# Linear attention and an ELU block on one core: scores of two heads as 64-row tiles, K^T V kept dense, both halves of a tile in one place

## The chip, the core and the metric

The kernel runs on one core of a Trainium2 chip. Its engines work side by side, each on its own queue of instructions and in order: PE (TensorE, matrix products), ACT (ScalarE), DVE (VectorE), POOL (GpSimd) and SP (which only starts transfers here). The metric is the time of one execution on the device in microseconds, from the median of several runs.

## The reference

```python
kv  = einsum('bhsd,bhse->bhde', k, v)          # 8 batches, 8 heads, 576 rows, head size 64
o   = einsum('bhsd,bhde->bhse', q, kv)
o   = o / sqrt(mean(o*o, over e) + 1e-6) * g_norm
x   = o with its heads side by side            # 4608 rows of 512
h   = x @ w_in                                 # 512 x 2048
g   = h if h > 0 else exp(h) - 1
out = g @ w_out                                # 2048 x 512
```

Inputs and output are float32; the kernel multiplies in bfloat16 and accumulates in float32.

## The kernel before, in words

The rows are worked off in nine tiles of 512. Tiles 0 to 7 take the first 512 rows of a batch each; tile 8 takes the last 64 rows of all eight batches. For each tile T there is an *attention* (its x, turned so that features lie on partitions: `xT`), a *first product* (h by eight steps `mm1`, each of eight matmuls that fill two banks of an accumulator `h_ps`), an *elu* (exponential on ACT, then `rest` on DVE: a step with min and subtract on `elu_e`, and one that takes the maximum with `h_ps` into `gT`), and a *second product* (`mm2`: 16 matmuls for each of four groups of 128 rows into `o_ps`, then a copy on ACT and a store from SP). With `relu` in an elu ACT also writes the positive part as bfloat16 (`elu_h`), which frees `h_ps` earlier, and DVE adds two bfloat16 operands.

Attention of tile T (function `attention`, line 249) is cut into pieces that the order of the program places among the steps of tile T-1's products:

- `kv` (`kv_single`, line 171): K^T V of batch T on PE, 72 matmuls of 64 rows by 64 columns. Two heads that share a pair (index l) stand on the two halves of the partitions. `kv_out` (line 352) casts the result with ACT into `bd_kv`, a block-diagonal tile: each pair of heads has a 128x128 block, of which the two off-diagonal quarters are zero. It takes one cast for each half of the partitions. The zeros come from a memset on DVE at the start (line 509).
- `qd` (line 261): a transposing transfer from SP that makes `qT`, queries with two heads on 128 partitions.
- `se0`, `se1` (`se_mm`, line 202): scores, here the product of q with K^T V, for 256 rows each. One matmul takes 128 partitions of `qT` (two heads) and a block of `bd_kv`, so that a matmul serves two heads at once, with half of what it multiplies being zeros. Eight matmuls fill the two banks of the accumulator `at`. In tile 8 each matmul has 64 output rows, since every 64 rows have their own batch. The same piece squares the result on ACT (line 227).
- `sum`, `inv`, `mul`: sums of squares by head on DVE (L232), logarithm and exponential on ACT for the root (L238, L239), and `scale_rows` on DVE (line 241), which writes `xs` in bfloat16.
- `xd0`, `xd1` (line 322): transposing transfers from SP of `xs` into `xT`; `xg0`, `xg1` (line 332) multiply `xT` by the gain vector on DVE. Attentions 1 and 2 use PE transposes instead (`x0`, `x1`, line 295). Tile 0 has a path of its own at the start, without `bd_kv`; a copy on POOL (L677) puts its K^T V there for tile 8.

The accumulator memory has eight banks: one tile `at` of two banks (pool `ps_at`, one buffer), two buffers of two banks for h (`ps_m1`), two of one bank for the second product (`ps_m2`). A pool hands out its buffers in turn, and the writer of a buffer waits for the last reader of the one before.

The order of each engine is the order in which the program is written (the kernel schedules by hand). `group` (line 728) writes out tiles 2 to 8: for i from 0 to 7 the i-th `mm1` of tile T, a piece of `mm2` of tile T-1, the `rest` of the elu, and the attention pieces whose start is i. From tile 3 on, the first eight matmuls of `mm2` stand ahead of the group, and the other seven pieces at i = 0 to 6. The starts are

```python
start = {"kv": 0, "se0": 1, "xd0": 2, "se1": 3, "xd1": 4, "xg0": 5, "xg1": 6}
```

with sum and inv of a half one step after its scores, and mul ahead of the other pieces there. Tile 1 is written out ahead of it (lines 757 to 777): attention 2 has `se0` after the seventh `mm1`, `se1` after eight matmuls of the second product. POOL's queue fetches q, k and v of later batches, each behind a small copy that waits for `qd`'s landing.

Of the kernel before, what the change touches and what calls it, by code (L numbers as in the profile page):

```python
# [8 lines left out]
FP32 = mybir.dt.float32  # L9
BF16 = mybir.dt.bfloat16  # L10
AF = mybir.ActivationFunctionType
ALU = mybir.AluOpType
# [4 lines left out]
def kernel(  # L17
# [13 lines left out]
    nc = tc.nc  # L31
    P = 128

    B, H, S, D = q.shape
    DM = H * D
# [25 lines left out]
    nc.vector.memset(eps_col, 1e-6)  # L61
    bd_kv = const.tile([P, B, NPAIR, P], BF16, name="bd_kv")

# [103 lines left out]
    def at_tile(dtype):  # L167
        full = ps_at.tile([P, 1024], FP32, name="at", tag="at")
        return full if dtype == FP32 else full.bitcast(BF16)
# [31 lines left out]

    def se_mm(T, j, qT, se_ps):

        ov = se_ps.rearrange("p (u l s e) -> p u l s e", u=2, l=2, s=2)
        for p in range(NPAIR):
            s, u = p // 2, p % 2
            if T < B:
                nc.tensor.matmul(  # L208
                    ov[:, u, :, s, :],
                    lhsT=qT(p, j),  # L210
                    rhs=bd_kv[:, T, p, :],
                    start=True,
                    stop=True,
                )
            else:
                for l in range(2):
                    nc.tensor.matmul(  # L217
                        ov[l * 64 : l * 64 + 64, u, :, s, :],
                        lhsT=qT(p, j)[:, l * 64 : l * 64 + 64],
                        rhs=bd_kv[:, 2 * j + l, p, :],  # L220
                        start=True,
                        stop=True,
                    )

# [15 lines left out]

    def scale_rows(xs, se_ps, ss, n):
        nc.vector.tensor_tensor(  # L242
            out=xs.rearrange("p c (h e) -> p (c h) e", h=H),
            in0=se_ps.rearrange("p c (h e) -> p (c h) e", h=H),
            in1=ss.to_broadcast([P, n * H, D]),
            op=ALU.mult,
        )

    def attention(T):
# [19 lines left out]

        def se(h):  # L270


            def product(se_ps=None):
                if se_ps is None:
                    se_ps = at_tile(FP32).rearrange("p (c f) -> p c f", c=2)
                for c in range(2):
                    se_mm(T, 2 * h + c, st["qT"], se_ps[:, c, :])
                st["se", h] = se_ps
                st["sq", h] = square(se_ps, 2)

            def sums():
                st["ss", h] = sum_heads(st.pop(("sq", h)), 2)

            def inv():
                inv_rms(st["ss", h])

            def scale():
                if h == 0:
                    st["xs"] = attp.tile([P, J, DM], BF16, name="xs", tag="xs")
                rows = st["xs"][:, 2 * h : 2 * h + 2, :]  # L290
                scale_rows(rows, st.pop(("se", h)), st.pop(("ss", h)), 2)

            return product, sums, inv, scale

# [57 lines left out]
        def kv_out(us):  # L352
            bd_v = bd_kv[:, T].rearrange("p (s u) e -> p s u e", s=2)
            for l in range(2):
                ls = slice(l * 64, l * 64 + 64)
                nc.scalar.copy(  # L356
                    bd_v[ls, :, us, ls],
                    st["kv"][ls, :, 0:P].rearrange("p s (u e) -> p s u e", u=2)[:, :, us],
                )

# [6 lines left out]

        pieces = {"kv": kv_all, "q": q_t, "qd": q_dma}
        pieces["landed"] = lambda: after(st["at"])
# [5 lines left out]
        for h in range(2):  # L375
            for name, piece in zip(("se", "sum", "inv", "mul"), se(h)):
                pieces[f"{name}{h}"] = piece
# [85 lines left out]
    def mm2_quarter(T, j, i):  # L463
        mm2(T, j, 4 * i, 4 * i + 4)
# [43 lines left out]
    nc.vector.memset(one, 1.0)  # L508
    nc.vector.memset(bd_kv, 0.0)
    fetch_q(0)  # L510
# [158 lines left out]
    for i in range(2, 8):  # L669
# [3 lines left out]
        if i == 5:  # L673
            at["q"]()
    for l in range(2):
        ls = slice(l * 64, l * 64 + 64)
        nc.gpsimd.tensor_copy(  # L677
            out=bd_kv[ls, 0].rearrange("p (s u) e -> p u s e", s=2)[:, :, :, ls], in_=kv0[ls]
        )
    load_w_out(3)  # L680
# [12 lines left out]
    at["kv1"]()  # L693
    at["se0"]()
    at["se1"](wide)
    for n in range(2):
# [30 lines left out]

    def group(T, at, start, second, relu=()):


        early, late = {}, {}
        for name, i in start.items():
            if name in ("se0", "se1"):
                early.setdefault(i + 1, []).extend(("sum" + name[2], "inv" + name[2]))
                late.setdefault(i + 1, []).insert(0, "mul" + name[2])
            late.setdefault(i, []).append(name)
        for i in range(9 if 8 in early else 8):
            if i == 8:
                for name in early[8] + late[8]:
                    at[name]()  # L740
                break
            rest = mm1(
                T, i, (slice(0, 512),), i in relu, between=[at[name] for name in early.get(i, ())]
            )
            for piece in second.get(i, ()):
                mm2(*piece)
            names = late.get(i, [])
            if i in relu and names[:1] in (["mul0"], ["mul1"]):
                at[names.pop(0)]()
            rest()  # L750
            for name in names:
                at[name]()

# [4 lines left out]
    for i in range(8):  # L758
        rest = mm1(1, i, relu=i in (1, 4), spare=i in (2, 5))
        rest()  # L760
        if i == 3:
            at["kv"]()
        if i == 6:
            at["se0"]()
    mm2(1, 0, 0, 8)
    at["se1"](ps_m1.tile([P, 2, G], FP32, name="se_ps", tag="mm1"))
    for n in range(2):
# [5 lines left out]
    mm2(1, 1, 0, FC)  # L773
    at["x0"]()
    at["x1"](ps_m1.tile([P, 2, G], FP32, name="xt_ps", tag="mm1")[:, 0, :])
    mm2_quarter(1, 2, 0)
    mm2_quarter(1, 2, 1)

    for T in range(2, NT):
        second = {i: [(T - 1, i // 2, 8 * (i % 2), 8 * (i % 2) + 8)] for i in range(8)}  # L780
        if T > 2:
            mm2(*second[0][0])
            second = {i - 1: second[i] for i in range(1, 8)}
        else:
            quarters = [(1, 2 + i // 4, 4 * (i % 4), 4 * (i % 4) + 4) for i in range(2, 8)]
            second = {i + 1: [piece] for i, piece in enumerate(quarters)}
        at, start = ahead, {}
        if T + 1 < NT:
            start = {"kv": 0, "se0": 1, "xd0": 2, "se1": 3, "xd1": 4, "xg0": 5, "xg1": 6}
        if T + 2 < NT:  # L790
            at["landed"]()
            fetch(T + 2)
            ahead = attention(T + 2)
        group(T, at, start, second, (1, 2, 4) if T == 2 else ())
        if T + 2 < NT:
            ahead["qd"]()
# [48 lines left out]
```

## Time and profile before

| what | us |
|---|---|
| median of 6 runs | 287.15 (286.98 to 287.46) |
| the profiled execution, its own time | 286.98 |
| its span, first to last instruction | 285.2 |
| PE busy | 277.6 |
| DVE busy | 168.3 |
| ACT busy | 144.0 |
| POOL busy | 53.1 |

The granted clock of PE is 0.999 of its full speed. Lines of the profile name the source line, the engine, the operation, the written and read tiles and their shapes; a number of instructions stands behind an x, then busy time and the mean length of one, then the time in which the engine was idle before them and what ended it. Matmuls overlap, so the mean length of one (379 ns for 512 moving columns) is more than the distance between two starts. PEld is the loading of the stationary operand, which runs beside PE. In this chip's profile K^T V is L177, the scores are L208 (L217 in tile 8), h is L399 and the second product L446 (L804 for the last tile).

### The profile page before, as it was taken

What the parts mean: (1) busy time and instruction counts of PE and PEld (TensorE: products, weight loads), DVE (VectorE), ACT (ScalarE), POOL (GpSimd) and SP (SyncE); (2) the same over time, 40 slices, a digit from 0 to 9 for tenths busy, and PEclk for the clock granted to TensorE, in tenths of its full rate; (3) what the DMA queues carried; (4) which work ended last, traced back from release to release, by engine and by line L of the source; (5) the groups of instructions that cost most, each with busy time, mean ns of one, the idle gap of its engine ahead of it and who ended that gap; (6) DMA issues with size and microseconds to landing.
All of it is one profiled execution on the core that took longest, in us unless ns stands there. A gap on an engine that the chain in (4) does not pass through costs nothing.

```text
span 285.2 us, 4859 instructions
## 1 busy us (share of the span) xinstructions
PE 277.6 (97%) x2001; PEld 133.3 (47%) x2001; DVE 168.3 (59%) x220; ACT 144.0 (50%) x205; POOL 53.1 (19%) x94
## 2 busy tenths in 40 slices
PE   6999899999999999999999999999999999999994
PEld 2544454445544444445444544454444444444444
DVE  5459461778378657655865577547764776444400
ACT  3779554785486455335543454455434553333311
POOL 7835302431431231005100520011000000000000
PEclk9999999999999999999999999999999999999999
DMA  7999999796992597168915892545150213010122
GB/s 198 206 204 203 206 205 165 222 170 126 180 175 57 150 176 173 37 149 113 239 37 151 106 227 56 150 98 153 34 143 16 97 28 99 0 76 0 74 74 74
DMA packets 55961, 35.96 MB, mean 126 GB/s; under 512 B 32772, under 2 KB 53508, under 8 KB 55940
## 3 DMA queue, kind: packets, MB, share of 16 engines
q0 software_dynamic: 20192, 17.30, 39.3%
q1 hardware_dynamic: 35348, 17.83, 24.3%
q10 hardware_dynamic: 400, 0.52, 0.5%
q8 instruction: 15, 0.25, 0.3%
q14 instruction: 6, 0.05, 0.1%
HBM read 36.70 MB, written 9.44 MB: 162 GB/s over the span
## 4 chain that ended last, share of the span: by engine, by line
PE 88%; DMA 10%; issue 0%; ACT 0%; POOLq 0%
PE h_ps L399 39%; PE o_ps L446 39%; DMA w_out_sb<-in_moe_w_out_dram 6%; PE o_ps L804 5%; DMA w_in_sb<-in_moe_w_in_dram 3%; DMA k_pk<-in_k_dram 2%; PE at L208 2%; PE at L177 2%; PE at L306 0%; PE at L217 0%; PE se_ps L208 0%; ACT bd_kv L356 0%; PE xt_ps L306 0%; ACT o_last L812 0%; POOLq L829 0%
## 5 line engine op out<-in xcount | busy, mean ns | idle before, releaser
L399 PE MATMUL h_ps<-xT,w_in_sb 128*128 128x512 bf16 x560 | 130.9, 379 | 0.0
L446 PE MATMUL o_ps<-w_out_sb,gT 128*128 128x512 bf16 x512 | 120.5, 379 | 0.2 <-DMA w_out_sb<-in_moe_w_out_dram 0.2
L411 ACT ACTIVATE elu_e<-h_ps 128x1024 bf16<-128x1024 f32 (+1 forms) x75 | 73.0, 982 | 81.8 <-PE h_ps L399 80.1
L399 PEld LDWEIGHTS <-w_in_sb 128*128 128x128 bf16 x560 | 53.5, 98 | 62.0 <-issue 0.2
L430 DVE TENSOR_TENSOR gT<-elu_e,h_ps 128x1024 bf16<-128x1024 bf16 (+1 forms) x66 | 76.3, 1156 | 6.9
L446 PEld LDWEIGHTS <-gT 128*128 128x128 bf16 x512 | 49.8, 98 | 59.3 <-DMA w_out_sb<-in_moe_w_out_dram 0.3
L422 DVE TENSOR_SCALAR elu_e<-elu_e 128x1024 bf16<-128x1024 bf16 (+1 forms) x76 | 32.2, 423 | 71.2 <-ACT elu_e L411 71.1
L459 ACT COPY o_sb<-o_ps 128x512 f32<-128x512 f32 x32 | 18.6, 587 | 16.6 <-PE o_ps L446 16.6
L232 DVE TENSOR_REDUCE ss<-sq 128x16 f32<-128x1024 bf16 x16 | 19.3, 1218 | 9.0 <-ACT sq L227 9.0
L227 ACT ACTIVATE sq<-at 128x1024 bf16<-128x1024 f32 x14 | 14.3, 1024 | 12.4 <-PE at L208 9.9
L151 POOL COPY q_bf<-q_pk 128x512 bf16<-128x512 bf16 x24 | 14.5, 632 | 28.0 <-DMA q_pk<-in_q_dram 28.0
L242 DVE TENSOR_TENSOR xs<-at,ss 128x1024 bf16<-128x1024 f32 x14 | 17.1, 1218 | 1.2 <-ACT ss L239 1.2
L804 PE MATMUL o_ps<-w_out_sb,gT 128*128 128x512 bf16 (+1 forms) x80 | 14.1, 337 | 0.0
L125 POOL COPY gate<-qT 1x1 bf16<-1x1 bf16 x6 | 1.2, 194 | 63.9 <-DMA qT<-q_bf 63.9
L104 POOL DMA_DIRECT2D q_pk<-in_q_dram x14 | 10.6, 765 | 3.1 <-issue 1.8
L804 PEld LDWEIGHTS <-gT 128*128 128x128 bf16 x80 | 7.7, 98 | 6.4 <-DVE gT L430 0.4
L118 POOL DMA_DIRECT2D k_pk<-in_k_dram x12 | 8.3, 694 | 5.3 <-DMA w_in_sb<-in_moe_w_in_dram 2.5
L417 ACT ACTIVATE elu_h<-h_ps 128x1024 bf16<-128x1024 f32 x9 | 9.2, 1019 | 0.0
L208 PEld LDWEIGHTS <-qT 128*128 128x128 bf16 x112 | 7.3, 98 | 3.5 <-issue 0.5
L118 POOL DMA_DIRECT2D v_pk<-in_v_dram x12 | 8.3, 689 | 2.3 <-DMA w_in_sb<-in_moe_w_in_dram 1.8
L177 PEld LDWEIGHTS <-k_pk 64*64 64x64 bf16 x576 | 6.5, 107 | 4.0 <-issue 3.8
L527 PE MATMUL bank<-zeros 128*128 128x512 bf16 x19 | 6.8, 487 | 1.2 <-DVE zeros L502 1.2
(71 smaller groups left out, 112.4 us busy)
## 6 DMA issues: line engine op xcount, KB each, us to landing
out_dram<-o_sb SPq DMA_DIRECT2D x16, 512.0 KB, 3.0
q_pk<-in_q_dram POOLq DMA_DIRECT2D x14, 256.0 KB, 5.6
k_pk<-in_k_dram POOLq DMA_DIRECT2D x6, 576.0 KB, 8.4
v_pk<-in_v_dram POOLq DMA_DIRECT2D x6, 576.0 KB, 10.5
w_in_sb<-in_moe_w_in_dram POOLq DMA_DIRECT2D x4, 512.0 KB, 10.6
w_out_sb<-in_moe_w_out_dram POOLq DMA_DIRECT2D x4, 512.0 KB, 15.1
st_q<-in_q_dram SPq DMA_DIRECT2D x2, 512.0 KB, 4.6
st_q<-in_q_dram SPq DMA_DIRECT2D x16, 64.0 KB, 2.5
```

The source lines that it names most:

```text
L118: nc.gpsimd.dma_start(out=raw[name, b].rearrange("p h j d -> p h (j d)")[:, hs], in_=in_[:, hs])
L151: eng.tensor_copy(out=out_, in_=in_)
L227: nc.scalar.activation(sq, se_ps, AF.Square)
L232: nc.vector.reduce_sum(out=ss, in_=sq.rearrange("p c (h e) -> p (c h) e", h=H), axis=AX.X)
L242: nc.vector.tensor_tensor(out=xs.rearrange("p c (h e) -> p (c h) e", h=H), in0=se_ps.rearrange("p c (h e) -> p (c h) e", h=H), in1=ss.to_b ...
L399: nc.tensor.matmul(h_ps[a][:, cs], lhsT=w_in_sb[:, c, f * P : f * P + P], rhs=x(c, cs), start=(c == 0), stop=(c == KC - 1),)
L411: nc.scalar.activation(e[:, lo:hi, :], ps, AF.Exp)
L422: nc.vector.tensor_scalar(out=e[:, lo:hi, :], in0=e[:, lo:hi, :], scalar1=1.0, scalar2=1.0, op0=ALU.min, op1=ALU.subtract,)
L430: nc.vector.tensor_tensor(out=gT[T][:, 2 * i + lo : 2 * i + hi, :], in0=e[:, lo:hi, :], in1=h, op=ALU.add if relu else ALU.max,)
L446: nc.tensor.matmul(o_ps[T, j], lhsT=gT[T][:, f, j * P : j * P + P], rhs=w_out_sb[:, f, :], start=(f == 0), stop=(f == FC - 1),)
L459: nc.scalar.copy(o_sb[T][:, j % 2, :], o_ps.pop((T, j)))
L804: nc.tensor.matmul(ps, lhsT=gT[B][:, f, j * P : j * P + P], rhs=w_out_sb[:, f, cols], start=(f == 0), stop=(f == FC - 1),)
```

## The change

`bd_kv` becomes `kv_sb`, which holds K^T V without zeros: 64 columns for each pair, one head on each half of the partitions. `kv_out` is one cast over 128 partitions, POOL's copy for tile 0 is one instruction, and the memset is gone. A scores matmul now takes one head: 64 partitions of `qT` and 64 columns of `kv_sb`; the two heads of a pair write to two different banks. The output is ordered by head within the pair first, so `scale_rows` works in two instructions for each half and sorts the columns while it writes `xs`.

In tiles 3 to 7 both halves of the scores stand together, after the fourth `mm1`: one half in `at`, the other in the two banks of the second product, which ACT copies to `se_sb` at once; no piece of `mm2` stands at that step, and one more at the last. Sums, roots, scaling and the two transfers all stand at i = 4, the gain multiplications at i = 6 and 7. The elu of steps 4 and 5 uses `relu` there. In tile 1 both halves stand where `se1` stood, and the second set of PE transposes moves one quarter of `mm2` later. Tile 2 keeps its order. The diff, cut:

```diff
-    bd_kv = const.tile([P, B, NPAIR, P], BF16, name="bd_kv")
+    kv_sb = const.tile([P, B, NPAIR, D], BF16, name="kv_sb")
...
+    def se_mm(T, h, qT, banks):
+        for jj in range(2):
+            j = 2 * h + jj
+            for p in range(NPAIR):
+                s, u = p // 2, p % 2
+                for t in range(1 if T < B else 2):
+                    rows = slice(0, P) if T < B else slice(t * 64, t * 64 + 64)
+                    for l in range(2):
+                        ls = slice(l * 64, l * 64 + 64)
+                        nc.tensor.matmul(
+                            banks[l].rearrange("p (j u s e) -> p j u s e", j=2, u=2, s=2)[
+                                rows, jj, u, s, :
+                            ],
+                            lhsT=qT(p, j)[ls, rows],
+                            rhs=kv_sb[ls, T if T < B else 2 * j + t, p, :],
+                            start=True,
+                            stop=True,
+                        )
...
-    def scale_rows(xs, se_ps, ss, n):
-        nc.vector.tensor_tensor(
-            out=xs.rearrange("p c (h e) -> p (c h) e", h=H),
-            in0=se_ps.rearrange("p c (h e) -> p (c h) e", h=H),
-            in1=ss.to_broadcast([P, n * H, D]),
-            op=ALU.mult,
-        )
+    def scale_rows(xs, se, ss):
+        for l in range(2):
+            nc.vector.tensor_tensor(
+                out=xs.rearrange("p j (u l s e) -> p l j u s e", u=2, l=2, s=2)[:, l].rearrange(
+                    "p j u s e -> p (j u) s e"
+                ),
+                in0=se[:, l, :].rearrange("p (a s e) -> p a s e", s=2, e=D),
+                in1=ss[:, 8 * l : 8 * l + 8]
+                .rearrange("p (a s) -> p a s", s=2)
+                .to_broadcast([P, 4, 2, D]),
+                op=ALU.mult,
+            )
...
+        def se(homes):
+            for h, home in homes.items():
+                if home is None:
+                    home = at_tile(FP32).rearrange("p (l f) -> p l f", l=2)
+                pair = isinstance(home, list)
+                banks = home if pair else [home[:, l, :] for l in range(2)]
+                se_mm(T, h, st["qT"], banks)
+                if pair:
+                    home = attp.tile([P, 2, G], FP32, name="se_sb", tag="se_sb", bufs=1)
+                    for l in range(2):
+                        nc.scalar.copy(home[:, l, :], banks[l])
+                st["se", h] = home
...
         def kv_out(us):
-            bd_v = bd_kv[:, T].rearrange("p (s u) e -> p s u e", s=2)
-            for l in range(2):
-                ls = slice(l * 64, l * 64 + 64)
-                nc.scalar.copy(
-                    bd_v[ls, :, us, ls],
-                    st["kv"][ls, :, 0:P].rearrange("p s (u e) -> p s u e", u=2)[:, :, us],
-                )
+            nc.scalar.copy(
+                kv_sb[:, T].rearrange("p (s u) e -> p s u e", s=2)[:, :, us],
+                st["kv"][:, :, 0:P].rearrange("p s (u e) -> p s u e", u=2)[:, :, us],
+            )
...
-    nc.vector.memset(bd_kv, 0.0)
...
+    def group(T, at, lead, second, relu=()):
+        for piece in lead:
+            mm2(T - 1, *piece)
...
+        for i in range(8):
+            between = [at["sq1"], at["sum0"], at["inv0"], at["sum1"]] if at and i == 4 else ()
+            rest = mm1(T, i, relu=i in relu, between=between)
+            if at and i == 3:
+                at["se"]({0: None, 1: [ps_m2.tile([P, DM], FP32, name="se_ps", tag="mm2") for _ in range(2)]})
+                at["sq0"]()
             for piece in second.get(i, ()):
-                mm2(*piece)
+                mm2(T - 1, *piece)
+            if at and i == 4:
+                at["inv1"]()
+                for n in range(2):
+                    at[f"mul{n}"]()
+                    at[f"xd{n}"]()
             rest()
+            if at and i == 0:
+                at["kv"]()
+            if at and i > 5:
+                at[f"xg{i - 6}"]()
...
-        if i == 6:
-            at["se0"]()
     mm2(1, 0, 0, 8)
-    at["se1"](ps_m1.tile([P, 2, G], FP32, name="se_ps", tag="mm1"))
+    at["se"]({0: None, 1: ps_m1.tile([P, 2, G], FP32, name="se_ps", tag="mm1")})
+    for n in range(2):
+        at[f"sq{n}"]()
...
     at["x0"]()
+    mm2_quarter(1, 2, 0)
     at["x1"](ps_m1.tile([P, 2, G], FP32, name="xt_ps", tag="mm1")[:, 0, :])
-    mm2_quarter(1, 2, 0)
     mm2_quarter(1, 2, 1)
...
+        elif T < B:
+            lead, pieces, steps = halves[:1], halves[1:], (0, 1, 2, 4, 5, 6, 7)
+        else:
+            lead, pieces, steps = halves[:1], halves[1:], range(7)
+        second = {i: [piece] for i, piece in zip(steps, pieces)}
+        group(T, at, lead, second, {2: (1, 2, 4), B: ()}.get(T, (4, 5)))
```

## The prediction

> **What bounds the kernel now.** I read the busy shares first, then the chain that ended last, then that chain in order of time, then the groups.
>
> ```profile
> PE 277.6 (97%) x2001; PEld 133.3 (47%) x2001; DVE 168.3 (59%) x220; ACT 144.0 (50%) x205; POOL 53.1 (19%) x94
> ...
> PE 88%; DMA 10%; issue 0%; ACT 0%; POOLq 0%
> ```
>
> TensorE is the bound, and ACT and DVE have half their time free. The chain in time (start, length, what) says where the changed parts sit on it:
>
> ```profile
> 34.40 0.45 PE at L177 x36
> ...
> 35.14 0.27 ACT bd_kv L356
> ...
> 35.45 0.61 PE at L208 x8
> 36.06 0.45 PE se_ps L208 x8
> 36.51 5.19 PE o_ps L446 x24
> ...
> 98.80 0.71 PE at L177 x72
> 99.50 1.83 PE h_ps L399 x8
> ...
> 219.70 0.57 PE at L217 x16
> 220.27 1.83 PE h_ps L399 x8
> ```
>
> From 30.8 us on PE runs without a gap, except 0.65 us at 34.8 for the two casts of K^T V. So the end moves by what PE's own work gets shorter, less any new wait. Eight matmuls of scores take 0.45 us (56 ns each, no loss on either side). Around the 64-row products (L177) and the 64-column ones (L217) time is lost: the next h_ps row is 1.83 instead of 1.73. The groups of matmuls and weight loads, kept apart by shape:
>
> ```profile
> L208 PE MATMUL at<-bd_kv,qT 128*128 128x128 bf16 x96 | 7.3, 219 | 0.6 <-ACT bd_kv L356 0.6
> L177 PE MATMUL at<-v_pk,k_pk 64*64 64x64 bf16 x504 | 5.7, 194 | 0.0
> L217 PE MATMUL at<-bd_kv,qT 128*64 128x128 bf16 x32 | 1.3, 222 | 0.0
> ...
> L208 PEld LDWEIGHTS <-qT 128*128 128x128 bf16 x112 | 7.3, 98 | 3.5 <-issue 0.5 <-PE at L177 0.2
> L217 PEld LDWEIGHTS <-qT 128*64 128x64 bf16 x32 | 0.9, 109 | 0.8 <-issue 0.8
> ```
>
> Means are latencies; the rate is busy time by count: L208 76 ns, L177 11 ns, with the edges of each burst in it. Start to start, L177 runs four tiles in 32 ns.
>
> **The scores on TensorE.** For T below 8, 16 matmuls (128 rows, 128 moving columns) become 32 (64 rows, 64 moving columns), two row halves side by side in two banks. No row shows 64 rows by 128 columns. From below: a pair passes as fast as four tiles of L177, 64 columns in 32 ns, so 16 x 0.032 = 0.51 us. From above: nothing overlaps and each costs a whole slot of L208, 32 x 0.056 = 1.79 us. In between, the two load weights in parallel but a 128-column load fills a 56 ns slot: 0.90 us. I take 0.51, since L177 has the same moving length and alternates row halves the same way, and since a load of 128 columns lasts 98 ns where one of 64 columns lasts 109: loads of full width aren't the slow ones.
>
> To this comes a change of tiling. Before L177 the first start comes 309 ns after the last 128-row matmul instead of 216, and the 72 matmuls with both edges hold PE for 0.81 us (0.71, and the 0.10 of the row behind), of which 18 rounds of 33 ns are 0.59: 0.22 us for the edges. L217 gives the same: 0.57 + 0.10 = 0.67 us, of which eight pairs of 56 ns are 0.45. The present L208 pays nothing. So a block of both halves costs 0.51 + 0.22 = 0.73 us against 0.90, a gain of 0.17. Tile 8 becomes 64 matmuls of L177's own form, 16 rounds of 33 ns: 0.53 + 0.22 = 0.75, against 2 x 0.67 = 1.35, a gain of 0.60.
>
> Here a rule of the Trainium skill speaks against the change. TensorEngine Tiling, Instruction Overhead, gives each matmul about 60 cycles however short it is, with the advice not to tile a dimension that is already small. At the 2.4 GHz of the skill's TensorE: Matmul & The Clock Gate (its first table) that is an estimated 25 ns, and 32 x 25 ns = 0.80 us, with the edges 1.02: 0.12 more per block. The row differs: 72 matmuls of 64 columns in 0.59 us are 8 ns each. The row decides; the rule's sum is with the rivals.
>
> **Tile by tile.** *Attention 1* (at 34.9): one cast instead of two in sequence takes 0.27 us off PE's wait, and the block costs 0.51 and one edge of 0.11, against 0.90: together 0.55 us. But the next work is the second quarter of the second product, which needs the second slice of w_out. It was issued at 22.91, and the shortest of the four landings, 13.4 us, is this one: 36.31. PE starts there at 36.35 already, 65 ns after the matmul before it instead of 56. The gain ends in a wait for that DMA: 0, at best 0.55 if it lands earlier, and nothing suggests that it does, as the DMA engines are full until then.
>
> *Attention 2*: both halves stand together after the first eight matmuls of the second product. PE gains 0.17. The last step before the next tile now has less cover: the second set of transposes is followed by one quarter (0.86 us) instead of two. DVE starts on it 0.20 us after the last transpose, needs 0.75 (its row now), and 0.05 pass until PE starts: 1.00 against 0.86, a wait of 0.14. Its xs is there in time: squares from 0.55 us after the block's start, sums and the four scalings end by 70.3, and PE asks at 71.1. Net gain 0.03.
>
> *Attention 3* keeps two blocks: 2 x (0.25 + 0.22) = 0.94 against 0.90, a loss of 0.04.
>
> *Attentions 4 to 7*: 4 x 0.17 = 0.68. *Attention 8*: 0.60.
>
> **What else these groups change, walked through.** Zero is the start of a group's first eight matmuls; eight are 1.73 us. Matmuls of h: the third row ends at 11.2, the fourth at 14.6, scores 14.6 to 15.4, fifth to 17.1, sixth 20.5, seventh 24.0, eighth 27.4; then two rows of the second product, and the next tile's first at 30.9. The pair's banks are free when ACT has copied the second output (0.59 us, from 13.1): by 13.7. ACT then: exponential 14.8 to 15.9, two copies to 16.8 (L459's 587 ns each), square, exponential to 18.7, square to 19.6, roots 0.5, relu to 21.0, roots, exponential, relu to 23.4. The bank that the second product wants at 17.1 is free at 16.4; the buffers of h at 22.3 and 25.7 are free at 21.0 and 23.4. DVE: sums end at 19.0 and 20.9; four scalings of 512 elements (0.69 each; a 128x512 copy of float32 out of the accumulator takes 691 ns) from 20.8 to 23.3; then the delayed elu steps, two of them on the short form (0.69 instead of 1.22). It has caught up at 27.6 and next gets work at 28.7: 1.1 us in reserve. The two transposes are issued at 22.2 and 23.4 and land 3.0 us later, 4.9 at worst, ahead of 27.1 and 30.4 where they are read. ACT has 14.2 us of work in 29.3 now; 2 x 0.59 + 2 x 1.02 less one cast of 0.37 make 17.0. All this is hidden. SP's order stays, and the transposing transfer of the next query, queued on SP behind the last store of the group, starts about 1.5 us later, with POOL's fetches behind it: they have 20 us to spare.
>
> One piece isn't hidden: the gain vector is multiplied into the second half of xT after the eighth elu, no longer before it, and PE's next h waits for it. The timeline around such an end, as it is now:
>
> ```profile
> 121.06 1.89 PE L399 MATMUL h_ps<-xT,w_in_sb 128*128 128x512 bf16 x8
> ...
> 122.78 1.89 PE L446 MATMUL o_ps<-w_out_sb,gT 128*128 128x512 bf16 x8
> 122.98 1.02 ACT L411 ACTIVATE elu_e<-h_ps 128x1024 bf16<-128x1024 f32 x1 [1.14 <-PE h_ps L399]
> 124.04 0.43 DVE L422 TENSOR_SCALAR elu_e<-elu_e 128x1024 bf16<-128x1024 bf16 x1 [1.30 <-ACT elu_e L411]
> 124.57 1.22 DVE L430 TENSOR_TENSOR gT<-elu_e,h_ps 128x1024 bf16<-128x1024 bf16 x1
> ```
>
> From the end of the eighth h: 0.20 to the exponential, 1.06 to DVE, 0.53 to the addition, 1.14 to the next on DVE (117.67 to 118.81), 0.48 for the multiplication, 0.05 to PE: 3.46 us. The cover is two rows, 3.45. I put 0.03 us on each of the five boundaries (tiles 4 to 8), 0.15 in all: nothing is left in reserve there.
>
> Costed at nothing: the cleared memset of the block-diagonal tile (1.77 us on DVE at the start; DVE waits for the query's DMA after it), POOL's one copy less (0.46 us; the last slice of w_out follows it, lands at 41.4 and is needed at 44.3), the casts of other tiles (ACT's free half).
>
> **Sum.** 0 + 0.03 - 0.04 + 0.68 + 0.60 - 0.15 = 1.12 us less. The profiled execution took 286.98 us (span 285.2, 1.8 around it), which becomes 285.9; the median of the runs, 287.15, lies 0.17 above it: 286.0.
>
> **Rivals.** *Weights bound the pairs.* The Trainium skill, TensorE: Matmul & The Clock Gate, section LDWEIGHTS, says that a load costs by its columns and not its rows: 32 loads of 128 columns instead of 16. The 98 ns rows sit under 56 ns slots, so the trace bounds a load at 56 and no lower. A pair at 56 ns makes a block 0.90 + 0.22 = 1.12: attention 2 loses 0.22 + 0.14, attention 3 0.90 + 0.44 - 0.90 = 0.44, the next four 0.88, attention 8 still gains 0.60, boundaries 0.15; 1.2 slower, 288.4. It is the one on the other side; it decides from about 43 ns a pair, where the sum is nil. The 25 ns rule comes to the same place: 0.26 + 0.34 + 0.48 + 0.47 (64 x 25 ns + 0.22 - 1.35) + 0.15 = 1.7 slower, 288.9. Both together are this case. Against it: 8 ns in L177, and 98 under 109.
>
> *Row halves don't overlap* (56 ns each): a block is 2.01, so 1.1 more for attentions 2 and 4 to 7, 1.3 for 3, 0.7 for 1, 0.6 less for 8, and 0.3 of waits: 7.2 slower, 294.4. Against it: L177 overlaps them.
>
> *The boundary becomes a wait.* If the chain of 3.46 us is 0.2 to 0.3 longer (DVE steps of 0.62 and 0.74 instead of 0.43 occur beside POOL's work; the four scalings use up the 1.1), five boundaries cost 1.0 to 1.5 and the sum is about nil: 287.2. For it: no reserve. Against it: POOL is idle there.
>
> *More than the sum*: edges cost less for row halves alone (0.22 less for seven blocks), or attention 1 keeps its 0.55: 284.6.
>
> **How the numbers follow.** Main case 0.57, weights or issue 0.17, boundary 0.14, no overlap 0.05, more 0.07. About 0.57 us (0.2%) is what this measurement can tell from no change. Main (285.4 to 286.5, of which 0.5 is faster and 0.07 the same) and "more" give faster 0.58 with a little of the boundary case; same 0.14; slower 0.28. Predicted 286.0. For 8 in 10 I go from 285.0 to 288.6: beyond lie most of "more", the case without overlap and part of the weights case.
>
> **What would show it.** Scores of a block 16 pairs at 32 ns, with 0.09 us ahead of them and 0.1 after; at 56 ns the weights case holds. PE waits on xT at five boundaries of under 0.1 us; more is the boundary case. A wait of some 0.4 to 0.5 us on w_out near 36 us, and one on xT of about 0.14 near 72 us. Transposes landing after 27 us of the group, or waits of PE on the accumulators, would show that my walk is wrong.

## The result: 0.4% faster, by the steps foreseen

The changed kernel takes 285.8 us in the median (285.5 to 287.6), beside 287.27 for the kernel before in the same series. The ratio is 0.9957, with an interval of 0.9948 to 0.9965: 1.2 us less, at least 1.0 and at most 1.5. (The medians lie 1.5 apart; the ratio is that of the means, in which two of the changed kernel's executions at a granted clock of 0.988 weigh.) The span went from 285.2 to 283.9 us, the profiled execution from 286.98 to 285.9. That is some twice what can be told from no change (0.57 us), so its parts can only be read from the trace, where an undisturbed tile repeats within 0.02 us; medians serve for whole kernels.

The busy shares after, and the shares of the chain by engine:

```profile
PE 276.4 (97%) x2145; PEld 130.1 (46%) x2145; DVE 161.1 (57%) x235; ACT 152.9 (54%) x217; POOL 53.0 (19%) x93
PE 86%; DMA 11%; POOL 1%; issue 0%; ACT 0%; POOLq 0%
```

PE has 144 matmuls more and is busy 1.2 us less. ACT is up 9 us and DVE down 7; neither is on the chain. The chain in order of time (start, length, what), cut to the places that the prediction named:

```profile
23.24 13.20 DMA w_out_sb<-in_moe_w_out_dram
36.48 5.34 PE o_ps L453 x24
...
72.72 1.89 PE h_ps L406 x8
...
98.94 0.71 PE at L177 x72
...
108.38 0.34 PE at L212 x16
108.72 0.23 PE se_ps L212 x16
108.96 1.83 PE h_ps L406 x8
...
124.60 1.75 PE h_ps L406 x8
...
128.08 0.70 PE at L177 x72
...
224.13 0.37 PE at L212 x32
224.51 0.27 PE se_ps L212 x32
224.77 1.83 PE h_ps L406 x8
```

L212 is the scores now, in two rows since its halves go to `at` and `se_ps`. At 108.38 a block of both halves takes 0.34 + 0.23 us, and the h row behind it is 1.83 instead of 1.73: 0.67 as the rows are rounded, 0.68 from the starts in the trace, against 0.90 for two L208 rows before. The second half is 16 matmuls, eight pairs, in 0.23: 29 ns a pair. The first half is 0.11 longer than the second, and this is the edge in front. Tile 8 (224.13) comes to 0.37 + 0.27 + 0.10 = 0.74.

Of the other places, the product at 36.48 had waited for the second slice of w_out, which landed at 36.43 (36.31 before). At 72.72 an h row takes 1.89, since PE waited 0.15 for `xT` (attention 2). The row at 124.60 is the first after a tile's end, 1.75 instead of 1.73: one boundary.

The groups of the new matmuls and of their weight loads, shapes apart (busy time and mean length, then idle time ahead), with the second product:

```profile
L453 PE MATMUL o_ps<-w_out_sb,gT 128*128 128x512 bf16 x512 | 119.8, 379 | 0.7 <-DMA w_out_sb<-in_moe_w_out_dram 0.7
L212 PEld LDWEIGHTS <-qT 64*128 64x128 bf16 x224 | 3.8, 95 | 3.4 <-issue 2.9 <-DVE elu_e L429 0.4
L212 PE MATMUL at<-kv_sb,qT 64*128 64x64 bf16 x128 | 3.3, 191 | 0.4 <-ACT kv_sb L363 0.4
L212 PE MATMUL se_ps<-kv_sb,qT 64*128 64x64 bf16 x96 | 2.4, 190 | 0.0
```

There were 112 weight loads of 7.3 us; the 224 loads take 3.8. Apart from the wait on w_out (0.7, was 0.2) and the one on the cast of K^T V (0.4, was 0.6) no wait of PE stands before the scores and the second product.

Where the 1.3 us of span come from can be read at the starts of K^T V (the L177 rows of the chain; the last row is the first start in the trace), which divide the kernel into one stretch for each attention:

| start of | before | after | since the row above |
|---|---|---|---|
| K^T V in tile 1 | 54.67 | 54.80 | +0.13 (attention 1 and the wait on w_out) |
| K^T V in tile 2 | 74.54 | 74.61 | -0.06 (attention 2) |
| K^T V in tile 3 | 98.80 | 98.94 | +0.07 (attention 3) |
| K^T V in tile 4 | 128.13 | 128.08 | -0.19 (attention 4) |
| K^T V in tile 5 | 157.46 | 157.22 | -0.19 (attention 5) |
| K^T V in tile 6 | 186.79 | 186.36 | -0.19 (attention 6) |
| the last second product | 267.51 | 266.18 | -0.90 (attentions 7 and 8) |

From there to the end both take the same time. The last row holds 0.19 for attention 7 and 0.58 for attention 8; the remaining 0.13 are a pause at 187.3 us inside the K^T V of tile 6 in the kernel before (its row is 0.83 long instead of 0.71), which no wait explains. It isn't an accident of one execution: three of the experiments' kernels have it at the same place, one of the kernel before with less of w_out (0.83) and two of the changed one (0.86 with the tiles alone, 0.85 with eight pads). As it comes with and without the tiles and the order, the change can't be credited with it.

### The profile page after: what moved, and what is told of

Read it like the earlier page. It is cut to its first block, busy times and chain, and to the rows that moved or that the text cites. A ratio compares the mean times of both kernels' runs of the same rounds, so it can differ in the third digit from the quotient of the medians.

```text
span 283.9 us, 5177 instructions
## 1 busy us (share of the span) xinstructions
PE 276.4 (97%) x2145; PEld 130.1 (46%) x2145; DVE 161.1 (57%) x235; ACT 152.9 (54%) x217; POOL 53.0 (19%) x93
## 4 chain that ended last, share of the span: by engine, by line
PE 86%; DMA 11%; POOL 1%; issue 0%; ACT 0%; POOLq 0%
PE h_ps L406 40%; PE o_ps L453 38%; PE o_ps L825 5%; DMA w_in_sb<-in_moe_w_in_dram 5%; DMA w_out_sb<-in_moe_w_out_dram 5%; DMA k_pk<-in_k_dram 2%; PE at L177 1%; PE at L212 1%; POOL w_in_sb L137 1%; PE se_ps L212 1%; PE at L316 0%; PE xt_ps L316 0%; ACT o_last L833 0%; POOLq L850 0%
## 5 line engine op out<-in xcount | busy, mean ns | idle before, releaser
L437 DVE TENSOR_TENSOR gT<-elu_e,h_ps 128x1024 bf16<-128x1024 bf16 (+1 forms) x56 | 64.1, 1145 | 5.8
L229 DVE TENSOR_REDUCE ss<-sq 128x16 f32<-128x1024 bf16 x16 | 19.3, 1218 | 8.2 <-ACT sq L224 7.4
L424 ACT ACTIVATE elu_h<-h_ps 128x1024 bf16<-128x1024 f32 x19 | 19.3, 1015 | 0.0
L437 DVE TENSOR_TENSOR gT<-elu_e,elu_h 128x1024 bf16<-128x1024 bf16 x19 | 13.2, 693 | 3.5 <-ACT elu_h L424 2.4
L240 DVE TENSOR_TENSOR xs<-at,ss 128x512 bf16<-128x512 f32 x18 | 11.5, 682 | 1.2 <-ACT ss L236 1.2
L224 ACT ACTIVATE sq<-at 128x1024 bf16<-128x1024 f32 x9 | 9.4, 1043 | 1.5 <-PE at L212 1.5
L833 ACT COPY o_last<-o_ps 128x512 f32<-128x512 f32 (+1 forms) x5 | 2.5, 501 | 10.8 <-PE o_ps L825 10.8
```

Source lines behind the costliest of these rows:

```text
L229: nc.vector.reduce_sum(out=ss, in_=sq.rearrange("p c (h e) -> p (c h) e", h=H), axis=AX.X)
L240: nc.vector.tensor_tensor(out=xs.rearrange("p j (u l s e) -> p l j u s e", u=2, l=2, s=2)[:, l].rearrange("p j u s e -> p (j u) s e"), in0 ...
L424: nc.scalar.activation(h[:, lo:hi, :], ps, AF.Relu)
L437: nc.vector.tensor_tensor(out=gT[T][:, 2 * i + lo : 2 * i + hi, :], in0=e[:, lo:hi, :], in1=h, op=ALU.add if relu else ALU.max,)
```

## The experiments

My theory was the prediction's: pairs overlap at some 32 ns, each change of tiling costs 0.22 us, attention 1's gain ends in the wait for w_out, DVE has 1.1 us in reserve in the middle of a group and nothing at its end. The rivals were that weights or issue set the pace of the pairs, that the tiles alone bring the gain (or the order alone), and that another wait lies close by.

**Tiles without the order.** 64-row tiles and dense K^T V, with the places of the scores as before: each tile has two half blocks instead of one block.

```diff
-        if T == 2:
+        if True:
             for i in range(8):
                 n = i // 2 - 1
...
-    at["se"]({0: None, 1: ps_m1.tile([P, 2, G], FP32, name="se_ps", tag="mm1")})
+        if i == 6:
+            at["se"]({0: None})
+    at["se"]({1: ps_m1.tile([P, 2, G], FP32, name="se_ps", tag="mm1")})
```

> The 64-row tiles and the dense K^T V of the changed kernel, in the order of work of the kernel before (scores of the two halves apart, no pair, no copy out, gain multiplications at steps 5 and 6). Theory (the tiles gain 0.22 us a block only because two blocks are one, since each block pays about 0.22 us for the change of tiling): attentions 2 to 7 gain nothing, attention 8 gains 1.35 - 2 x 0.48 = 0.39, attention 1 ends at the landing of w_out; 0.4 us faster than before, 0.8 to 0.9 slower than the changed kernel. Rival (the tiles alone are the gain, the new order only brings its waits): 1.2 us or more faster than before.

Measured: 287.62 us, ratio 1.0015 (1.0002 to 1.0028). So the rival that the tiles bring the gain by themselves falls. The starts of K^T V in tiles 3 to 6 are 29.33 us apart, as in the kernel before: a half block alone takes 0.34 + 0.10 = 0.45, exactly what eight full-width matmuls of 56 ns took. In tile 8 two bursts of 0.48 replace two of 0.67, a gain of 0.38. The total missed my figure by 0.7, and the trace shows 0.67 of it in three places that I had not reckoned with: w_out's second slice landed at 36.55 (0.24 later than before), a matmul in tile 2 started 0.08 late, and the last product took 14.15 us to its last start instead of 13.80. The timeline there:

```profile
268.71 0.43 DVE L429 TENSOR_SCALAR elu_e<-elu_e 128x1024 bf16<-128x1024 bf16 x1 [1.70 <-ACT elu_e L418]
269.59 1.22 DVE L437 TENSOR_TENSOR gT<-elu_e,h_ps 128x1024 bf16<-128x1024 bf16 x1 [0.46 <-DVE elu_e L429]
270.87 1.90 PE L809 MATMUL o_ps<-w_out_sb,gT 128*128 128x512 bf16 x8 [0.23 <-DVE gT L437]
```

DVE stood still for 0.46 us between two instructions of its own, with the operands there; in the changed kernel the same gap is 0.10, and PE starts only 0.05 late.

**The order without the tiles.** Block-diagonal matmuls, with both halves together and copied out as in the change.

```diff
+                if T < B:
+                    nc.tensor.matmul(
+                        ov[:, u, :, s, :],
+                        lhsT=qT(p, j),
+                        rhs=bd_kv[:, T, p, :],
...
```

> The new order (both halves together, pair in the accumulators of the second product and copied out, relu at steps 4 and 5, new places of the multiplications) with the block-diagonal tile and the 128-row matmuls of before. Theory (the order itself gains nothing where a block pays no edges): attention 2 loses 0.14 to 0.16 on its wait, the five boundaries 0.02 each, attention 8 gains one pair of edges, 0.22; together within 0.1 us of before. Rival (the order relieves waits by itself): 0.5 us or more faster than before.

Measured: 287.52 us, ratio 1.0002 (0.9987 to 1.0018). A block of full-width matmuls takes 0.89 in one place as in two, and the starts of K^T V are 29.35 to 29.36 apart, so each boundary costs 0.02. Attention 2's wait of 0.15 is there too; tile 8 gains 0.23, one pair of edges. The order alone brings nothing. With the tiles alone bringing nothing for attentions 4 to 7 either, the gain there is of both together: the tiles make the matmuls cheap, and the order pays for one change of tiling instead of two.

**One head after the other.** The same matmuls, first all of a pair's first head, then all of the second, so that neighbours use the same row half.

```diff
-        for jj in range(2):
-            j = 2 * h + jj
-            for p in range(NPAIR):
...
-                    for l in range(2):
-                        ls = slice(l * 64, l * 64 + 64)
+        for l in range(2):
+            ls = slice(l * 64, l * 64 + 64)
+            for jj in range(2):
+                j = 2 * h + jj
...
```

> The changed kernel with the scores of a half in the other order: all matmuls of the first head of the pairs, then all of the second, so that neighbours no longer use different row halves. Theory (two row halves overlap, 29 ns a pair): each of 32 matmuls takes its own 29 ns, 0.46 us more for each of attentions 2 to 7, about the same for 8, attention 1 hides its part in the wait for w_out: 2.8 to 3.3 us slower than the changed kernel. Rival (the pace is the issue of instructions, some 15 ns each, whatever their place): no difference. Second rival (the loads bind when they aim at one half): 56 ns each, 1.3 us a block, 9 us slower.

Measured: 286.92 us, ratio 0.9974 (0.9951 to 0.9998); the last product starts 1.07 us later than with the change. The chain, with a half block of attention 3 and the block of attention 4:

```profile
78.12 0.47 PE at L212 x16
...
108.58 0.38 PE at L212 x13
108.96 0.02 PE se_ps L212
108.98 0.01 PE at L212
...
109.05 0.27 PE se_ps L212 x13
109.32 1.83 PE h_ps L406 x8
```

A half takes 0.47 us instead of 0.34, a block 0.74 instead of 0.57. Neighbours on the same row half start 29 ns apart; with the change, where they are on different ones, the two of a pair start 3 ns apart. So it is the overlap of matmuls on different row halves that makes the pair cheap (neighbours here also write to the same bank, where the change's pair writes to two, so this run alone doesn't separate row half and bank): issue as the limit would have made no difference, and weight loads of 56 ns are excluded by 29. The size was off by a factor of three, because where the heads change PE doesn't finish one before the other. For three matmuls the starts come alternately 8 to 12 and 17 to 21 ns apart, and the rows at 108.96 show `se_ps` and `at` taking turns, though all 16 matmuls of `at` stand ahead of those of `se_ps` in the program. A half costs 13 steps of 29 ns instead of 16. So PE seems to start a matmul of the other row half ahead of a queued one of the same half; the record has no row half in it, so that part is inferred from the times and the tile names.

**Pads on DVE.** A memset of 0.27 us in attentions of tiles 4 to 8, either ahead of the last multiplication with the gain vector or in the middle of the group; three and eight of them there.

```diff
+            if at and i == 7:
+                nc.vector.memset(pad, 0.0)
             if at and i > 5:
                 at[f"xg{i - 6}"]()
```

> The changed kernel with one memset of 512 bfloat16 columns (0.27 us, of no use) on DVE between the eighth elu and the last gain multiplication of tiles 3 to 7. Theory (nothing in reserve at the five boundaries): each wait on xT grows from 0.02 to 0.23 to 0.29 us, 1.0 to 1.4 us slower. Rival (PE has some reserve there and the 0.02 is no wait on xT): no difference.

```diff
             if at and i == 4:
                 at["inv1"]()
+                for _ in range(3):
+                    nc.vector.memset(pad, 0.0)
```

> The changed kernel with three memsets of 512 bfloat16 columns (0.27 us each, about 0.7 to 0.8 us together, of no use) on DVE ahead of the four scalings at step 4 of tiles 3 to 7. Theory (1.1 us in reserve on DVE between step 4 and the eighth elu): no difference, within 0.15 us of the changed kernel, though the work is three times that of the pad at the end. Rival (no reserve on DVE anywhere): 5 x 0.75, 3.5 to 4 us slower.

and with eight in place of three:

> The same with eight memsets, 1.8 to 2.2 us. Theory (1.1 us in reserve): what exceeds it comes out as a wait on xT at each of five boundaries, 0.7 to 1.1 us each, 3.5 to 5.5 us slower than the changed kernel. Rival (DVE isn't what PE waits for): no difference.

| kernel | us | ratio | K^T V to K^T V |
|---|---|---|---|
| one at the end | 286.82 | 0.9981 (0.9962 to 1.0001) | 29.30 |
| three in the middle | 285.95 | 0.9954 (0.9941 to 0.9967) | 29.14 |
| eight in the middle | 294.48 | 1.0272 (1.0224 to 1.0320) | 30.86 |

The changed kernel has 29.14. The one at the end costs 0.16 at each boundary, at once: there is no reserve, as the prediction said. It is less than I expected because the instruction behind the pad took 0.36 us in place of 0.48, so that the pad delayed the end by 0.16 only. Three in the middle took 1.05 us of DVE and cost nothing. Eight took more than I had reckoned:

```profile
114.53 3.01 DVE L769 MEMSET pad<- 128x256 uint32 x8
...
126.25 1.90 PE L406 MATMUL h_ps<-xT,w_in_sb 128*128 128x512 bf16 x8 [1.56 <-DVE xT L344]
```

Of 3.0 us, 1.7 came through in each tile: the reserve is 1.3 us (predicted 1.1). The expectation's total was low because it put 0.22 to 0.27 on each pad, where eight in a row took 0.38 each (0.27 of it busy).

**Without the two reliefs.** The change frees PE's accumulators early in two ways, which the prediction costed as hidden work: `relu` in two elus, and the copy of one half to `se_sb`. The first experiment drops `relu`, the second lets DVE read the half from the accumulators.

```diff
-        group(T, at, lead, second, {2: (1, 2, 4), B: ()}.get(T, (4, 5)))
+        group(T, at, lead, second, {2: (1, 2, 4)}.get(T, ()))
```

> The changed kernel without the relu form of the elu at steps 4 and 5 of tiles 3 to 7, so DVE reads h from the accumulator there. Theory (the relu matters because it frees the accumulator of h ahead of the scalings): the seventh h waits for the fifth elu's addition, which comes after the four scalings: 2 to 3 us for each of five tiles, 10 to 15 us slower. Rival (it only saves 1.1 us of DVE time, which the reserve covers): under 1 us slower.

```diff
                 if pair:
-                    home = attp.tile([P, 2, G], FP32, name="se_sb", tag="se_sb", bufs=1)
-                    for l in range(2):
-                        nc.scalar.copy(home[:, l, :], banks[l])
+                    home = banks
```

> The changed kernel without the copy out: the second half of the scores stays in the two banks of the second product until it is scaled (its square is taken in two instructions). Theory: the second product at step 4 waits for a bank until the last scaling, some 6 us after it is wanted, in each of five tiles, 25 to 32 us slower. Rival (the wait is short as PE has other work): under 5 us.

Measured: 305.86 us (ratio 1.0644, 1.0613 to 1.0675) and 322.81 us (1.1233, 1.1211 to 1.1256). The waits themselves are as expected; the list of waits (us in total, how many, the longest) has for the one and the other

```profile
PE h_ps L406 <- DVE gT L437: 13.2, 5, 2.9
```

```profile
PE o_ps L455 <- DVE xs L244: 25.7, 5, 5.1
```

but the spans grew by 19.3 and 36.7 us. Most of the rest is what a wait can leave behind. The timeline without `relu`:

```profile
118.84 2.76 PE L406 MATMUL h_ps<-xT,w_in_sb 128*128 128x512 bf16 x8 [2.58 <-DVE gT L437]
121.39 2.75 PE L453 MATMUL o_ps<-w_out_sb,gT 128*128 128x512 bf16 x8
123.98 1.89 PE L406 MATMUL h_ps<-xT,w_in_sb 128*128 128x512 bf16 x8
```

After a wait of 2.58 us the next two rows of eight matmuls take 2.55 and 2.59 us from start to start instead of 1.73, and the granted clock over these two rows is 0.67 and 0.66. Without `relu` this follows three of the five waits and costs 1.7 us each; after the other two, which are about as long, the clock stays at 1.00. Without the copy it follows all five, and the mean granted clock of the whole execution is 0.955 (0.983 without `relu`). With eight pads, where the waits are 1.6 us, it is 1.000. So the change rests on both reliefs: without either, the order of the change would be 6 or 12% slower than the kernel before.

**The wait on w_out.** To see whether attention 1's gain really ends in that wait, I fetch half of w_out's first slice only and clear the rest with a memset, in both kernels (half of that slice's weights are zeros in these two, so part of the second product is left out). The second slice then lands 1.2 us earlier, at 35.2.

```diff
-        fs = slice(4 * s, 4 * s + 4)
+        fs = slice(4 * s, 4 * s + (2 if s == 0 else 4))
...
+    nc.vector.memset(w_out_sb[:, 2:4, :], 0.0)
```

The kernel before:

> The kernel before with half of the first slice of w_out left out (two of its four blocks are zeros from a memset on DVE, not fetched), so that all later transfers of that queue land about 1.3 us earlier. Theory (PE is 0.05 us behind w_out's second slice by chance of the sizes): only the 0.20 us wait on the first slice goes, 0.2 us faster than before.

The kernel after:

> The changed kernel with the same half left out. Theory (0.55 us gained at attention 1 end in the wait for w_out's second slice): both waits on w_out go, 0.7 us in the changed kernel's profile, so 0.5 to 0.7 us faster than the changed kernel and 1.6 to 1.8 faster than the kernel before with the same half left out. Rival (the stretch is bound by something else too): 0.2 us faster, as in the kernel before.

Measured: 287.31 us (ratio 0.9993, 0.9970 to 1.0016) and 285.10 us (0.9905, 0.9868 to 0.9943). The kernel before gains nothing from the earlier landing; the changed one gains 0.7. From one to the other, K^T V of tile 1 starts at 54.60 and 54.07: 0.53 us earlier, where the prediction put attention 1's hidden gain at 0.55. The wait had taken all of it.

**Covers put back.** Three places where the change lost something, mended: the second slice of w_out is issued before the keys and values of the batch behind it and attention 1 stands a quarter later; the transposes of attention 2 stand half a quarter earlier; the last gain multiplication stands ahead of the eighth elu.

```diff
     load_w_out(0)
+    load_w_out(1)
...
     for j in order:
         mm2_quarter(0, j, 0)
+    for j in order:
+        mm2_quarter(0, j, 1)
     at["kv1"]()
...
+            if at and i == 7:
+                at["xg1"]()
             rest()
...
-    mm2_quarter(1, 2, 0)
+    mm2(1, 2, 0, 2)
     at["x1"](ps_m1.tile([P, 2, G], FP32, name="xt_ps", tag="mm1")[:, 0, :])
+    mm2(1, 2, 2, 4)
```

> The changed kernel with three covers: w_out's second slice fetched ahead of the second halves of k and v of batch 1 and its products ahead of attention 1's last K^T V; two matmuls ahead of attention 2's second transposes and six behind, instead of none and four; the last gain multiplication ahead of the eighth elu's DVE steps. Theory: the waits of about 0.4 on w_out, 0.16 at attention 2 and 5 x 0.02 at the boundaries go: 0.6 to 0.8 us faster than the changed kernel, about 285.1. Rival (the transfers bind that stretch whatever their order): 0.2 us faster.

Measured: 286.04 us, ratio 0.9947 (0.9915 to 0.9978). The boundaries are gone (29.12 between K^T V, from 29.14) and attention 2's wait too (19.65 from 19.81). But K^T V of tile 1 starts at 55.09, 0.29 later than with the change. In place of the wait on w_out (0.4) there are others, by PE's starts 0.2 us for the first scaling and 0.5 for ACT to read the transposes out of `at`, which both sets of transposes use. So a second version writes the second set to another accumulator and stands the first behind all of the fourth quarter of two row groups (the diff is against the version above):

```diff
-    mm2(0, 2, 12, FC, hold=True)
-    at["x0"]()
-    mm2(0, 3, 12, FC, hold=True)
+    for j in order[:2]:
+        mm2(0, j, 12, FC, hold=True)
     mm2_out(0, 2)
     mm2_out(0, 3)
-    at["x1"]()
+    at["x0"]()
+    mm2(0, 0, 12, FC)
+    at["x1"](ps_m1.tile([P, 2, G], FP32, name="xt_ps", tag="mm1")[:, 0, :])
     unpack_q(2, Q)
     ahead["qd"]()
-    for j in order[2:]:
-        mm2(0, j, 12, FC)
+    mm2(0, 1, 12, FC)
```

> As e10, with another end of tile 0: both remaining products that need the shared accumulator go ahead of attention 1's first transposes, and the second transposes write to a free accumulator of h, after one more piece of the second product. Theory (in e10 the waits of 0.43 for the first scaling and 0.50 for a reader of the shared accumulator took the place of the one on w_out): the step from the fourth quarter to tile 1 keeps 0.4 to 0.5 us, attention 2 another 0.15, the five boundaries 0.10; 0.5 to 0.75 us faster than the changed kernel, about 285.2. Rival (the stretch is bound by the landings of w_out and v): no faster than e10.

Measured: 285.75 us, ratio 0.9935 (0.9912 to 0.9958), no different from the change within its interval. The trace has the gain and its loss: the last product starts at 265.75 instead of 266.18, 0.43 earlier, and then takes 14.15 us instead of 13.80, with the same idle 0.46 us between two DVE instructions as in the first experiment. This pause appears in two of the kernels, at the same instruction, and not in the others; a transfer of instructions (8 KB) starts 0.7 us after it in both, and one lies there without a pause in the changed kernel. What sets it is open.

## Point by point

- *Pairs overlap at the pace of L177's tiles.* Right. Predicted 32 ns a pair, measured 29; the block 0.68 where 0.73 stood, so a gain of 0.21 instead of 0.17. This is the term that was mis-sized, and with four attentions it is most of what the sum lacked. The 25 ns for each matmul that I had estimated from the Trainium skill's 60 cycles (TensorEngine Tiling, Instruction Overhead) and set against the row would make a pair 50 ns. The 29 here are 14.5 for each, and in tile 8 64 matmuls pass in 0.53 us, 8 ns each. So the measured starts decide against the estimate here.
- *Each change of tiling costs 0.22.* Right: 0.11 ahead and 0.10 behind. The half blocks of attention 3 take 0.45 each, so that its predicted loss of 0.04 is nil by these terms; the stretch lost 0.07 in a start at 91.9 us that is 0.19 late (0.11 before), which no wait explains.
- *Weights as the bound* (the likeliest rival): falls. 128-column loads on two row halves sit under 29 ns a pair.
- *Attention 1's gain ends in the wait on w_out.* Right, and shown by fetching less: with the slice there, 0.53 us appear. Without that, it was 0.13 worse than nil, as the slice landed 0.12 later; the prediction had no reason for that term, nor have I now.
- *Attention 2*: 0.03 predicted, 0.06 measured. The wait is 0.15 (predicted 0.14), and the block's gain larger.
- *Attentions 4 to 7 with their boundaries*: 0.14 each predicted, 0.19 measured. A boundary costs 0.02 instead of 0.03 (29.14 between K^T V, where the version without boundaries has 29.12). That it has no reserve is shown by the pad at the end.
- *Attention 8*: 0.60 gained as predicted, 0.745 a block where 0.75 stood.
- *The walk through a group.* Right where it can be read: the scalings of attention 4, in tile 3's group, end at 116.84 us (23.25 from the group's start, predicted 23.3), DVE has caught up 27.5 into the group (27.6) and has its next work at 28.65 (28.7). The reserve is 1.3 us by the pads (predicted 1.1). ACT's work in the group went from 14.2 to 16.5 us (predicted 17.0). `relu` and the copy hide the rest, and cost 20 and 37 us where they are missing.
- *The timeline at a tile's end*, from which the boundary was taken, now:

```profile
121.19 1.02 ACT L418 ACTIVATE elu_e<-h_ps 128x1024 bf16<-128x1024 f32 x1 [2.43 <-PE h_ps L406]
122.24 0.43 DVE L429 TENSOR_SCALAR elu_e<-elu_e 128x1024 bf16<-128x1024 bf16 x1 [1.14 <-ACT elu_e L418]
122.78 1.22 DVE L437 TENSOR_TENSOR gT<-elu_e,h_ps 128x1024 bf16<-128x1024 bf16 x1
123.91 0.48 DVE L344 TENSOR_SCALAR xT<-xT,g_col 128x1024 bf16<-128x1024 bf16 x1
124.45 1.90 PE L406 MATMUL h_ps<-xT,w_in_sb 128*128 128x512 bf16 x8
```

The multiplication L344 stands behind the eighth elu, and PE's next h starts at its end, each step at the distance that the prediction gave it.

The sum was 1.12 us; by the same terms as measured it is -0.13 + 0.06 - 0.07 + 4 x 0.19 + 0.58 = 1.20, and 0.13 more is the late start in the kernel before. So the prediction of 286.0 was right for its reasons. That the sum came within 0.1 us of its measured terms is in part luck: attentions 4 to 7 brought 0.20 more than their terms and attention 1 0.13 less, for unrelated reasons.

## What to carry to other kernels

A short burst of matmuls in another tiling pays some 0.2 us for going in and out, so join bursts before making them cheaper: here eight pairs alone gained nothing, and sixteen together gained a quarter of the block. A gain just ahead of a wait for a transfer is worth nothing until the transfer lands earlier, so look what PE asks for next before counting it. And before moving an accumulator's readers together, count who frees the banks: one missing copy turned a gain of 1.2 us into a loss of 35.

## What the runs showed of the hardware beyond that

- Matmuls of 64 rows by 128 columns with 64 moving start 29 ns apart on the same row half and bank, and 3 ns apart on different ones. The overlap also comes about between matmuls that aren't neighbours in the program (13 steps instead of 16 in a half block).
- Waits on PE can lower the granted clock afterwards: after three of five waits of 2.5 to 2.9 us, and after all five of 5.1 us. Two rows of 1.73 us become 2.55 and 2.59 after a shorter one, 3.37 and 2.63 after a longer. Taken together, the five waits of each kernel lengthened its span by about one and a half times their own sum (13.2 us became 19.3, 25.7 became 36.7). Waits of 1.6 us left the clock at 1.000.
- Pauses of 0.1 to 0.46 us between two instructions of one engine, without a wait that explains them, lie at places that differ from kernel to kernel (inside the K^T V of tile 6 in four of the fourteen kernels, near 91.9 us in tile 2, the last product in two experiments). They are as large as the single terms of this sum, and their cause is open.
